# A transformer block on one core: PV in either lane beside the last out projection, first MLP weights in four transfers, second ones later, and another planned order

## The chip, the cores and the metric

The kernel runs on one core of one Trainium2 chip. The metric is device time in microseconds (us) of one execution. The core's engines are named as in the profile: PE (TensorE, matmuls), PEld (its weight loads), ACT (ScalarE), DVE (VectorE), POOL (GpSimd) and SP (SyncE, which mostly issues DMA transfers). Each engine runs its own instruction list in order and waits at semaphores.

## The reference

Input x is 2048 x 512 in bf16. With 32 heads of 16 columns, one key and one value head shared by all of them, and a hidden width of 1792 it computes

```python
xn = layernorm(x)
q, k, v = xn @ wq, xn @ wk, xn @ wv           # q: 32 heads of 16; k, v: one head of 16
p = softmax(q @ k.T * 16 ** -0.5)             # 2048 x 2048 per head
s = concat_heads(p @ v) @ wo
g = silu(silu(xn @ w1) @ w2)
out = x + s * g
```

## The kernel before

A planner written in Python (`Planner`) simulates five engines with fixed costs while the kernel is being built, and writes each engine's instruction list in the order that it finds. Whatever the constants of the planner are, the device only sees the resulting order and the semaphore waits. Some constants are random: `SEEDS` has a number for every 6 us of planned time (`STRETCH`), and each draws other values of the priorities (`Mix`), so another list gives another order of the same kinds of work.

**Work.** The 2048 rows are 16 tiles of 128, or four chunks of 512 queries. The queries of eight heads in a chunk are one block of 128 rows (`qt_sb`, 16 blocks `oi`); a group `g` (32 of them) is four heads of a block, in two pairs `i`. A group has 64 score units, each 64 keys by 512 queries for the two heads of a pair. A unit is a PE step of four matmuls 64x32 (`score`, recorded at L1033 and L1039) into one of the eight PSUM banks. Its exponential is taken either by ACT (L1829, into `pa_sb`, one or two units at once) or by DVE, which writes bf16 bits of an approximation (L1124, into `db_sb`); for the latter three shifted copies are made (POOL at L1311 or DVE at L1307, into `ds_sb`), and their four weighted products with V are added. So an ACT unit needs one PV entry, a DVE unit four. PV (`do_pv`, L1393) collects the group's output and the softmax's sum in one PSUM bank; then DVE transposes, divides and transposes back (`make_norm`, L1414 to L1435) into `on_sb`.

**Lanes.** The 64x32 matmuls of a step take the array's rows in halves of 64; two steps with swapped halves run side by side. The planner calls these lane 0 and lane 1 (`tensor`, mode "U"). A score unit run in one lane has its PV entry fixed to the other lane (`u.lane`, `bt.lanes`), and `pv_half` takes only entries of the lane that asks (L1338).

**MLP.** For each chunk 14 jobs "h" (`mk_h`, products with `w1_sb`, ACT tanh and a DVE product into `u_sb`) and then four jobs "z" (`mk_z`, products of `u_sb` with `w2_sb`). A job's products run in both lanes between scores and PV. Jobs "w" are the out projection of finished chunks; for the last chunk there is a separate end.

**The end.** When all scores are assigned and no job is left, `make_tail` lists for each of four row tiles the first three eight-head blocks of the out projection, once per lane (`tail["half"]`, 12 steps of four matmuls in each lane, L1625). Lane 1 opens the accumulation of a row tile, and lane 0 may only follow when lane 1 has done its three steps for that tile (L1611). The fourth block (L634, full 128 rows) needs the last group's `on_sb` and starts only when lane 0's list is empty (L1635). Then come the products with g (L854 to L859), the sum with x and the stores.

**Transfers.** SP issues nearly all loads in one in-order queue: x tiles, wk, wv, wq, the rest of x, then `w1_sb` in one transfer of 1792 KB once the normalised tile 5 is placed (`W1_AT`, L499), `w2_sb` in 14 transfers of 128 KB, of which number k follows hidden block max(0, k - 3) of chunk 0 (L501), and wo. Between them it copies q (`add_q1`, L771) and V (`mk_V`, L737) to other partitions. The planner takes 250 bytes per ns for transfers (`place`, L182 to L185).

The lines that set which PV entry a lane may run, and when the last block starts:

```python
for ent in pvq[g][i]:
    if ent.lane != lane:
        continue
...
if l == 0 and any(q == r for q, _ in tail["half"][1]):
    return INF
...
if tail["half"][0]:
    return None
```

Of the kernel before, what the change touches and what calls it, by code (L numbers as in the profile page):

```python
# [22 lines left out]
SEEDS, STRETCH = [0, 621430, 964855, 634377, 64350, 0, 694092, 944034, 510981, 983451, 126593, 580856, 234150, 0, 405364, 0, 0, 639952, 236919, 380010, 794098, 385191, 672036, 0, 789095, 553358, 196796, 902258, 0, 0, 0, 514317, 0, 331162, 593301, 0, 0, 437315, 0, 0, 917832, 457243, 378342, 445316, 218187, 875070, 402692, 608418, 665513, 0, 0, 713570, 834070, 919202, 142859, 159991, 0, 53048, 725479, 111780, 0, 961704, 55976, 234814, 688798, 646486, 6388, 105124, 192922, 681295, 882883, 467008, 979031, 477536, 901050, 975096, 0, 0, 980853, 663567, 0, 620538, 913744, 251242, 618568, 299334, 120371, 0, 397467, 0, 362185, 47491, 718084, 0, 0, 0, 0, 0, 635882, 0, 0, 0, 0, 0, 0, 0, 0, 0, 0], 6000.0  # L23
STG = {2: 3, 3: 11}
# [84 lines left out]
class Planner:  # L109
# [47 lines left out]
    def place(self, eng, dur, emit, reads, writes, dma=0, t0=None, ports=1, after=None):  # L157
# [217 lines left out]
def bass_recurrent_scan__grouped_kv_mqa__dense_activation_silu__prompt_kernel(  # L375
# [29 lines left out]
    with ExitStack() as es:  # L405
# [71 lines left out]
        def xkey(t):  # L477
            return ("Ds", XB + t // BS, t % BS)
# [4 lines left out]
        for t in range(4):  # L483
            dma((SP, AC)[t % 2], "x", x_tile(t), xv[:, t, :], 128, [xkey(t)], prio=-2)
        dma(SP, "wk", wkv_sb[:, :, 0:DH], A_wk.rearrange("(dc p) e -> p dc e", p=P), 16, ["wk"], prio=0)
        dma(SP, "wv", wkv_sb[:, :, DH:2 * DH], A_wv.rearrange("(dc p) e -> p dc e", p=P), 16, ["wv"], prio=0)
        dma(SP, "wq", wq_sb[:], A_wq.rearrange("(dc p) n -> p dc n", p=P), 512, ["wq"], prio=0)
        for j in range(1, 4):
            dma(SP, "x", ds_sb[:, XB + 4 * j // BS, 4 * j % BS * NQ:(4 * j % BS + 4) * NQ].bitcast(BF16).rearrange("p (t d) -> p t d", d=D),
                xv[:, 4 * j:4 * j + 4, :], 512, [xkey(4 * j + h) for h in range(4)], prio=1)  # L490
# [80 lines left out]
        for j in range(4):  # L571
            for t in range(4 * j, 4 * j + 4):
                if t == 1:
                    continue
                ts_ = pl.add(Task(DV, 593.0, lambda v, t=t: v.bn_stats(stats_sb[:, t, :], x_tile(t)),  # L575
                                  [xkey(t)], [("st", t)], 1 + j,
                                  gate=(lambda j=j: xn_task[STG[j]].op is not None) if j > 1 else
                                  (lambda: ("xnT", 3) in pl.lastw) if j > 0 else None))
                pl.add(Task(DV, 66.0, lambda v, t=t: v.bn_aggr(mv_sb[:, t, :], stats_sb[:, t, :]),  # L579
                            [("st", t)], [("mv", t)], 1 + j, [ts_]))  # L580
# [242 lines left out]
        def mk_h(c, ft, pace):  # L823
            def consume(jb, op):
# [62 lines left out]
        def add_xr(tt):  # L887
            if tt < NT - 4:
# [4 lines left out]
            xr_task[tt] = pl.add(Task(SP, T_SP, lambda e: e.dma_start(xr_sb[:, tt % 4, :], xv[:, tt, :]),  # L893
                                      (), [("xr", tt % 4), "w1"], 2, [fin_task[tt - 4]], dma=128 * 1024))
            later(xr_task[tt], hidden(NC - 1, NFT - 1))
# [427 lines left out]
        def pv_half(t, lane):  # L1323
# [254 lines left out]

        tail = dict(made=False, items=[], sums=[], half=([], []), prev={})

        def make_tail():
            tail["made"] = True
            c = NC - 1
            for r in range(4):
                tt = 4 * c + r
                for o in range(NOC):
# [16 lines left out]

        def tail_half(l, t):
            if not tail["half"][l]:
# [9 lines left out]
            rr = pl.ready(PE, tail_reads(r, o), [("ps", tb[r])] if o == 0 and l == 1 else ())  # L1615
            if l == 0 and o == 0:
                rr = max(rr, pl.vis(tail["prev"][r], PE))
            if rr > t + 20:
                return rr
            tail["half"][l].pop(0)  # L1620

            def emit(pe):
                for j in range(4):
                    r0 = 64 * (j // 2 ^ l)
                    h = pe.matmul(bank(tb[r])[32 * j:32 * (j + 1), :],  # L1625
                                  lhsT=on_cols(oi % NON, slice(r0, r0 + 64), r * P + 32 * j, 32),
                                  rhs=wo_sb[r0:r0 + 64, o, :], start=o == 0 and l == 1, stop=False,
                                  tile_position=(r0, 32 * j), skip_group_check=True)
                return h
            tail["prev"][r] = pl.tensor("U", l, MM, emit, tail_reads(r, o), [("ps", tb[r])], t,  # L1630
                                        after=tail["prev"].get(r) if l == 0 and o == 0 else None)
# [329 lines left out]
```

## Time and profile before

| | before |
|---|---|
| median of 3 runs | 655.04 us (654.72 to 655.38) |
| the profiled execution's own time | 655.33 us |
| its span | 653.5 us |
| PE, DVE, ACT, POOL busy | 644.5, 632.8, 640.9, 578.6 us |
| first score matmul | 10.34 us |
| last exponential ends | 644.43 us |
| last block of the out projection starts | 647.40 us |
| granted TensorE clock | 1.0 |

The span runs from the first to the last instruction; the execution's time has 1.8 us more around it. A "group" is all instructions of one line, engine and shape. In a row of the timeline the first two numbers are start and length, and the bracket says how long the engine was idle before it and who ended that. "issue" is idle time with no releaser that the profile shows.

### The profile page before, as it was taken

The page shows a single profiled execution, that of the slowest core. Times are in us where ns is not written, and L with a number is a line of the kernel's source. Part 1 is how long each engine was busy: PE and PEld are TensorE (multiplying, and loading weights), DVE is VectorE, ACT ScalarE, POOL GpSimd, SP SyncE. Part 2 cuts the span into 40 slices and gives each one's busy share as a digit, 9 for nine tenths or more (in the row PEclk, how much of TensorE's full clock was granted, in tenths as well). Part 3 has the DMA queues.
Part 4 walks back from the last instruction along what each step waited for, and adds up shares of the span by engine and source line. Part 5 has one row for each costly group of instructions (what it writes and reads, how often), then busy time and mean ns, then how long its engine had stood idle before and what let it go on. Part 6 is the DMA issues. An engine that isn't in the chain of part 4 may idle for free.

```text
span 653.5 us, 44343 instructions
## 1 busy us (share of the span) xinstructions
PE 644.5 (99%) x22007; PEld 347.8 (53%) x19480; DVE 632.8 (97%) x1136; ACT 640.9 (98%) x1132; POOL 578.6 (89%) x331
## 2 busy tenths in 40 slices
PE   7999999999999999999999999999999999999997
PEld 3455656555555554554465555545555555475543
DVE  8999999999999999999999999999999999997995
ACT  7999999999999999999999999999999999999996
POOL 3068899999999999999989999999998999997961
PEclk9999999999999999999999999999999999999999
DMA  6521110000011210000000001000000001200001
GB/s 179 157 66 34 38 42 21 11 5 10 13 35 36 37 34 14 10 5 4 11 5 10 13 13 27 4 5 10 6 10 5 10 14 21 51 4 6 4 3 36
DMA packets 12920, 16.57 MB, mean 25 GB/s; under 512 B 2432, under 2 KB 11904, under 8 KB 12544
## 3 DMA queue, kind: packets, MB, share of 16 engines
q1 hardware_dynamic: 10384, 11.31, 5.9%
q0 software_dynamic: 1920, 2.03, 2.3%
q8 instruction: 162, 2.65, 1.7%
q10 hardware_dynamic: 432, 0.39, 0.2%
q14 instruction: 22, 0.18, 0.1%
HBM read 8.95 MB, written 3.67 MB: 19 GB/s over the span
## 4 chain that ended last, share of the span: by engine, by line
PE 96%; DVE 2%; DMA 1%; SPq 0%; issue 0%
PE ps L1393 33%; PE ps L1039 29%; PE ps L761 20%; PE ps L1033 13%; DMA ds_sb<-in_A_x_dram 1%; DVE stats_sb L575 1%; PE ps L650 1%; PE ps L1625 0%; PE ps L685 0%; SPq L474 0%; PE ps L723 0%; DVE w_sb L856 0%; DVE xn_sb L611 0%; DVE mv_sb L579 0%; DVE w_sb L859 0%
## 5 line engine op out<-in xcount | busy, mean ns | idle before, releaser
L1829 ACT ACTIVATE pa_sb<-ps 128x512 bf16<-128x512 f32 (+1 forms) x1039 | 608.6, 771 | 2.7 <-PE ps L1039 1.9
L1311 POOL INT64_ADD ds_sb<-db_sb x299 | 563.7, 1958 | 33.4 <-PE ps L1393 12.4
L1124 DVE TENSOR_SCALAR db_sb<-ps 128x512 uint16<-128x512 f32 x794 | 494.8, 682 | 6.3 <-PE ps L1039 3.7
L1039 PE MATMUL ps<-qt_sb,kt_sb 64*32 64x512 bf16 x5664 | 481.4, 378 | 1.0 <-ACT pa_sb L1829 0.6
L1393 PE MATMUL ps<-ds_sb,v_sb 64*32 64x512 bf16 x4872 | 359.4, 376 | 0.0
L1393 PE MATMUL ps<-pa_sb,v_sb 64*32 64x512 bf16 x2472 | 258.0, 377 | 0.0
L1033 PE MATMUL ps<-qt_sb,kt_sb 64*32 64x512 bf16 x2528 | 244.2, 375 | 0.8 <-DMA qt_sb<-qt_sb 0.5
L1039 PEld LDWEIGHTS ps<-qt_sb,kt_sb 64*32 64x32 bf16 x5664 | 136.3, 89 | 150.0 <-ACT pa_sb L1829 65.4
L1393 PE MATMUL ps<-db_sb,v_sb 64*32 64x512 bf16 x1624 | 189.5, 376 | 0.0
L1393 PEld LDWEIGHTS ps<-ds_sb,v_sb 64*32 64x32 bf16 x4872 | 140.6, 91 | 41.8 <-issue 12.1
L761 PE MATMUL ps<-xnT_sb,w_sb 64*32 64x512 bf16 x1792 | 133.7, 377 | 0.4 <-issue 0.4
L761 PE MATMUL ps<-w_sb,u_sb 64*32 64x512 bf16 x1792 | 132.7, 377 | 0.0
L1393 PEld LDWEIGHTS ps<-pa_sb,v_sb 64*32 64x32 bf16 x2472 | 87.9, 91 | 28.2 <-issue 10.2
L1393 PEld LDWEIGHTS ps<-db_sb,v_sb 64*32 64x32 bf16 x1624 | 62.1, 91 | 13.0 <-issue 3.4
L761 PEld LDWEIGHTS ps<-xnT_sb,w_sb 64*32 64x32 bf16 x1792 | 44.2, 91 | 24.4 <-issue 6.0
L761 PEld LDWEIGHTS ps<-w_sb,u_sb 64*32 64x32 bf16 x1792 | 44.5, 91 | 17.3 <-issue 4.0
L817 ACT ACTIVATE t_sb<-ps 128x512 bf16<-128x512 f32 x72 | 48.8, 677 | 0.6 <-PE ps L761 0.5
L818 DVE SCALAR_TENSOR_TENSOR u_sb<-t_sb,ps 128x512 bf16<-128x512 bf16 x56 | 38.0, 679 | 0.6 <-ACT t_sb L817 0.2
L761 PE MATMUL ps<-xnT_sb,wq_sb 64*32 64x512 bf16 x480 | 36.1, 377 | 0.0
L761 PE MATMUL ps<-wo_sb,on_sb 64*32 64x512 bf16 x384 | 29.4, 377 | 0.0
L1414 DVE STREAM_TRANSPOSE ps<-ps 128x512 f32<-128x512 f32 (+1 forms) x33 | 23.2, 707 | 4.3 <-PE ps L1393 2.7
L1450 POOL DMA_DIRECT2D kt_sb<-kt_sb x4 | 2.3, 584 | 21.3 <-DVE kt_sb L703 16.0
(79 smaller groups left out, 197.0 us busy)
## 6 DMA issues: line engine op xcount, KB each, us to landing
w_sb<-in_B_w_dram SPq DMA_DIRECT2D x1, 1792.0 KB, 8.9
w_sb<-in_B_w_dram SPq DMA_DIRECT2D x14, 128.0 KB, 2.5
ds_sb<-in_A_x_dram SPq DMA_DIRECT2D x3, 512.0 KB, 6.5
qt_sb<-qt_sb SPq DMA_DIRECT2D x16, 96.0 KB, 2.1
out_dram<-in_A_x_dram SPq DMA_DIRECT2D x12, 128.0 KB, 2.5
out_dram<-ob_sb POOLq DMA_DIRECT2D x12, 128.0 KB, 3.1
v_sb<-v_sb SPq DMA_DIRECT2D x8, 80.0 KB, 2.2
wq_sb<-in_A_wq_dram SPq DMA_DIRECT2D x1, 512.0 KB, 4.6
```

Of the source, the lines that this page charges most:

```text
L575: ts_ = pl.add(Task(DV, 593.0, lambda v, t=t: v.bn_stats(stats_sb[:, t, :], x_tile(t)), [xkey(t)], [("st", t)], 1 + j, gate=(lambda j=j: x ...
L650: h = pe.transpose(dst[:, k, dc * P:(dc + 1) * P], xn_sb[:, t % 4, dc * P:(dc + 1) * P], ident[:, :])
L761: h = pe.matmul(bank(b)[32 * j:32 * (j + 1), :], lhsT=lhs(k, rows, 32 * j, 32), rhs=rhs(k, rows), start=first, stop=last, tile_position=(r ...
L817: t1 = Task(AC, T_AF + 0.8333 * NQ, lambda a: a.activation(t_sb[:, k, :], bank(b), ACT.Tanh, scale=scale), [("ps", b)], [("t", k)], 0)
L818: t2 = Task(DV, T_P, lambda v: v.scalar_tensor_tensor(out=dst, in0=t_sb[:, k, :], scalar=1.0, in1=bank(b), op0=ALU.add, op1=ALU.mult), [(" ...
L1033: h = pe.add_instruction(mybir.InstMatmult(name=pe.bass.get_next_instruction_name(), engine=mybir.EngineType.PE, ins=[pe.lower_ap(q), pe.l ...
L1039: h = pe.matmul(to, lhsT=keys, rhs=q, start=True, stop=True, tile_position=(r0, 32 * j), skip_group_check=True)
L1124: bt.P[k] = pl.add(Task(DV, T_P, lambda v: v.tensor_scalar(db_sb[:, bt.b, k * NQ:(k + 1) * NQ], bank(b), 128.0 * LOG2E, 128.0 * (SHIFT_BET ...
L1311: whole["po"].append(pl.add(Task(PO, 100.0 + (T_P64 - 100.0) * bt.n / BS, lambda g: g.int64_add(ds_sb[:, s, 0:n].bitcast(U64), db_sb[:, bt ...
L1393: h = pe.matmul(bank(OB)[q:q + 32, :], lhsT=lhs(rows), rhs=rhs[rows], start=s0, stop=s1, tile_position=(64 * l, q), skip_group_check=True)
L1414: t1 = pl.add(Task(DV, (T_TR - 60.0) / parts + 60.0, lambda v, cols=cols: v.transpose(bank(OB)[:, cols], bank(OB)[:, cols]), [("ps", OB)], ...
L1829: op = pl.place(AC, 0.8333 * NQ * n + T_AF, lambda a: a.activation(pa3[:, k0:k1 + 1:max(1, k1 - k0), :], ps3[:, b0:b1 + 1:step, :], ACT.Ex ...
```

## The change

1. In the end (`FLEX`), a PV entry may run in either lane once the tail is made. Lane 1 runs out projection steps while they are ready and lane 0 runs PV (`tail["at"]`); when lane 1's remaining steps and the remaining PV are no more than lane 0's steps, the roles are swapped once. Three of the row tiles (`HEADS`) are opened by lane 1 and the fourth by lane 0. The last block waits for both lists.
2. `w1_sb` comes in four transfers of 448 KB, one per block of 128 input columns. They follow normalised tiles 5, 8 and 10 and the K eviction of tile 7. A product round waits only for its own quarter.
3. Transfer k of `w2_sb` follows hidden block 4 + k // 2 of chunk 0.
4. The planner's transfer costs are other ones (360 bytes per ns, other sizes for small loads and V), and wq has another priority behind wk and wv, with the same place in the queue. `SEEDS` is another list of the same length (109), so the whole order is planned anew.

```diff
-W1_AT, SKIP = 5, 1877.999
+W1_AT, SKIP = (5, 8, 10, -7), 1877.999
...
-T_MS, V_AT = 500.0, 9
+T_MS, V_AT, W2_AT, FLEX, HEADS, SW_AT = 500.0, 9, 4, True, 3, 0
...
-T_V, T_VE, V_KB = 220.0, 410.0, 150
+T_V, T_VE, V_KB = 220.0, 410.0, 200
...
-T_SP, T_ST = 600.0, 480.0
+T_SP, T_ST, DMA_RATE, W_KB, WQ_AT, EARLY_ST = 600.0, 480.0, 360.0, 140, 1, 0
+X_KB = 128
...
-                self.dma_t = start + dma / 250.0
-            op.vis = start + dma / 250.0 + 600.0
+                self.dma_t = start + dma / DMA_RATE
+            op.vis = start + dma / DMA_RATE + 600.0
...
-        later(dma(SP, "w1", w1_sb[:], w1v, 1792, ["w1"], prio=2), lambda: xn_task.get(W1_AT))
+        for k in range(NDC):
+            later(dma(SP, "w1", w1_sb[:, k, :], w1v[:, k, :], 448, [("w1", k)], prio=2),
+                  (lambda k=k: xn_task.get(W1_AT[k])) if W1_AT[k] >= 0 else (lambda k=k: evac_kt.get(-W1_AT[k])))
         for k in range(NFT):
-            later(dma(SP, "w2", w2_sb[:, k, :], w2v[:, k, :], 128, [("w2", k)], prio=3), hidden(0, max(0, k - 3)))
+            later(dma(SP, "w2", w2_sb[:, k, :], w2v[:, k, :], 128, [("w2", k)], prio=3), hidden(0, W2_AT + k // 2))
...
-                    lambda k, rows: xnT_sb[rows, k, c * NQ:(c + 1) * NQ], lambda k: ["w1"] + xnT_keys(c))
+                    lambda k, rows: xnT_sb[rows, k, c * NQ:(c + 1) * NQ], lambda k: [("w1", k)] + xnT_keys(c))
...
+            if FLEX and tail["made"]:
+                if lane != tail["at"] and tail_half(lane, t, False) is True:
+                    return t + MM, None
+                rest = sum(max(tot[n, i] - done[n, i] for i in range(2)) for n in range(g, NG))
+                if lane == tail["at"] == 0 and len(tail["half"][1]) + rest <= len(tail["half"][0]) + SW_AT and tail_half(0, t, False) is True:
+                    tail["at"] = 1
+                    return t + MM, None
             for i in range(2):
                 for ent in pvq[g][i]:
-                    if ent.lane != lane:
+                    if ent.lane != lane and not (FLEX and tail["made"]):
                         continue
...
+            if FLEX:
+                tail["half"][0].sort(key=lambda x: (x[0] < HEADS, x[0], x[1]))
...
-            if l == 0 and any(q == r for q, _ in tail["half"][1]):
+            head = int(not FLEX or r < HEADS)
+            if l != head and any(q == r for q, _ in tail["half"][head]):
                 return INF
...
         def tail_round(t):
-            if tail["half"][0]:
+            if any(tail["half"]):
                 return None
```

More of the change, by code (lines that the diff above doesn't have):

```diff
@@ L577, in bass_recurrent_scan__grouped_kv_mqa__dense_activation_silu__prompt_kernel @@
                                   gate=(lambda j=j: xn_task[STG[j]].op is not None) if j > 1 else
-                                  (lambda: ("xnT", 3) in pl.lastw) if j > 0 else None))
+                                  (lambda t=t: ("xnT", 3) in pl.lastw or t < EARLY_ST and xn_task[3].op is not None) if j > 0 else None))
                 pl.add(Task(DV, 66.0, lambda v, t=t: v.bn_aggr(mv_sb[:, t, :], stats_sb[:, t, :]),
@@ L893, in add_xr @@
             xr_task[tt] = pl.add(Task(SP, T_SP, lambda e: e.dma_start(xr_sb[:, tt % 4, :], xv[:, tt, :]),
-                                      (), [("xr", tt % 4), "w1"], 2, [fin_task[tt - 4]], dma=128 * 1024))
+                                      (), [("xr", tt % 4)] + [("w1", k) for k in range(NDC)], 2, [fin_task[tt - 4]], dma=128 * 1024))
             later(xr_task[tt], hidden(NC - 1, NFT - 1))
@@ L1577, in tbk @@
             return tb[r]
-        tail = dict(made=False, items=[], sums=[], half=([], []), prev={})
+        tail = dict(made=False, items=[], sums=[], half=([], []), prev={}, at=0)
         def make_tail():
@@ L1602, in sum_key, with tail_half @@
             return ("fx", r) if r in EVR else ("fin", r % 2)
-        def tail_half(l, t):
+        def tail_half(l, t, go=True):
             if not tail["half"][l]:
@@ L1614, in tail_half @@
                 return INF
-            rr = pl.ready(PE, tail_reads(r, o), [("ps", tb[r])] if o == 0 and l == 1 else ())
-            if l == 0 and o == 0:
+            rr = pl.ready(PE, tail_reads(r, o), [("ps", tb[r])] if o == 0 and l == head else ())
+            if l != head and o == 0:
                 rr = max(rr, pl.vis(tail["prev"][r], PE))
@@ L1619, in tail_half @@
                 return rr
+            if not go:
+                return True
             tail["half"][l].pop(0)
@@ L1626, in emit @@
                                   lhsT=on_cols(oi % NON, slice(r0, r0 + 64), r * P + 32 * j, 32),
-                                  rhs=wo_sb[r0:r0 + 64, o, :], start=o == 0 and l == 1, stop=False,
+                                  rhs=wo_sb[r0:r0 + 64, o, :], start=o == 0 and l == head, stop=False,
                                   tile_position=(r0, 32 * j), skip_group_check=True)
@@ L1630, in tail_half @@
             tail["prev"][r] = pl.tensor("U", l, MM, emit, tail_reads(r, o), [("ps", tb[r])], t,
-                                        after=tail["prev"].get(r) if l == 0 and o == 0 else None)
+                                        after=tail["prev"].get(r) if l != head and o == 0 else None)
             return True
         def tail_round(t):
-            if tail["half"][0]:
+            if any(tail["half"]):
                 return None
```

11 lines of the change are left out of this document (6 added, 5 removed).

## The prediction

> **What bounds the kernel now.** I read the page's busy times and its chain of waits first, then the groups by form, then the windows of 16 us, and last the timeline of both ends.
>
> ```profile
> span 653.5 us, 44343 instructions
> PE 644.5 (99%) x22007; PEld 347.8 (53%) x19480; DVE 632.8 (97%) x1136; ACT 640.9 (98%) x1132; POOL 578.6 (89%) x331
> PE 96%; DVE 2%; DMA 1%; SPq 0%; issue 0%
> L1829 ACT ACTIVATE pa_sb<-ps 128x512 bf16<-128x512 f32 (+1 forms) x1039 | 608.6, 771 | 2.7 <-PE ps L1039 1.9
> L1039 PEld LDWEIGHTS ps<-qt_sb,kt_sb 64*32 64x32 bf16 x5664 | 136.3, 89 | 150.0 <-ACT pa_sb L1829 65.4
> ```
>
> The chain lies 96% on PE, but ScalarE (ACT) is 98% and VectorE (DVE) 97% busy, and the score weights wait longest for exponentials to free a PSUM bank. So three engines bound it together, and a gain must take work or idle time from all of them, or from the ends where only one works.
>
> ```profile
> L1829 ACT ACTIVATE pa_sb<-ps 128x512 bf16<-128x512 f32 x842 | 447.8, 693 | 2.4 <-PE ps L1039 1.9 <-PE ps L1033 0.5
> L1829 ACT ACTIVATE pa_sb<-ps 128x1024 bf16<-128x1024 f32 x197 | 207.2, 1104 | 0.3
> L1124 DVE TENSOR_SCALAR db_sb<-ps 128x512 uint16<-128x512 f32 x794 | 494.8, 682 | 6.3 <-PE ps L1039 3.7 <-PE ps L1033 0.5
> ```
>
> 842 + 2 x 197 = 1236 score units go through ACT, at 608.6 / 1236 = 0.49 us of ACT time each; a unit on DVE costs 494.8 / 794 = 0.62 us. An ACT unit is one PV entry of two matmuls; a DVE unit is four (one plus three shifted copies), so moving a unit to DVE costs PE six matmuls more.
>
> ```profile
> 32.00:48.00 16.00, 15.99 (x480) 7.92 (x428) 15.42 (x28) 14.83 (x27) 10.27 (x7) 1.00 0.22 61
> 240.00:256.00 16.00, 16.00 (x580) 7.68 (x504) 16.00 (x29) 16.00 (x33) 15.77 (x10) 1.00 0.12 21
> 592.00:608.00 16.00, 16.00 (x560) 8.17 (x488) 12.50 (x22) 16.00 (x28) 11.69 (x8) 1.00 0.02 5
> 608.00:624.00 16.00, 16.00 (x572) 9.21 (x495) 14.24 (x26) 16.00 (x30) 14.81 (x8) 1.00 0.02 5
> 624.00:640.00 16.00, 16.00 (x496) 7.04 (x396) 14.42 (x22) 16.00 (x23) 8.28 (x6) 1.00 0.01 3
> ```
>
> After the window come PE, weight loads, DVE, ACT and POOL. The middle is full: 580 matmuls per 16 us (36 per us) with no idle on DVE or ACT. Busy time hides a thin stretch on PE, since two half-arrays run side by side; the counts show it. The weak places are the start (480 matmuls, ACT idle 1.2 us) and the last three windows: DVE is idle 3.5 + 1.8 + 1.6 = 6.8 us, and (580 - 560) + (580 - 572) + (580 - 496) = 112 matmuls are missing, 112 / 36 = 3.1 us of PE. The clock is 1.00 throughout, so no clock effect enters.
>
> **Part 1, PV in either lane beside the out projection.** The end before:
>
> ```profile
> 640.82 3.61 ACT L1829 ACTIVATE pa_sb<-ps 128x1024 bf16<-128x1024 f32 x4
> 642.16 0.40 PE L1625 MATMUL ps<-wo_sb,on_sb 64*32 64x512 bf16 x4
> 644.48 0.10 PEld L1393 LDWEIGHTS ps<-pa_sb,v_sb 64*32 64x32 bf16 x4 [0.26 <-ACT pa_sb L1829]
> 644.55 2.93 PE L1625 MATMUL ps<-wo_sb,on_sb 64*32 64x512 bf16 x52
> 644.94 0.80 DVE L1414 STREAM_TRANSPOSE ps<-ps 128x256 f32<-128x256 f32 x2 [1.59 <-PE ps L1625]
> 646.25 0.49 DVE L1435 STREAM_TRANSPOSE on_sb<-otr_sb 128x128 f32<-128x128 f32 x2
> 647.40 0.56 PEld L634 LDWEIGHTS ps<-wo_sb,on_sb 128*32 128x32 bf16 x16 [0.42 <-issue]
> ```
>
> From 642.16 the out projection (L1625) has one lane and PV the other. The last PV waits for the last exponential (640.82 + 3.61 = 644.43). Then 52 matmuls, 13 steps of four, run one after another in one lane, (2.93 - 0.38) / 12 = 0.21 us each, with the other lane empty. The last round (L634) follows them at 647.40, although its input from DVE was done at 646.25 + 0.49 = 646.74.
>
> ```profile
> 642.40:644.90 2.50, 2.49 (x48) 0.97 (x40) 1.00 0.00 0
> ```
>
> That row is L1393 alone: 48 matmuls, 12 PV steps. With the new rule 12 PV steps and 24 projection steps fill both lanes: 36 x 0.21 / 2 = 3.8 us, done by about 646.0. Then DVE sets L634: 646.74 plus a hand-over of 0.05 (ACT's end at 644.43 to the load at 644.48), so 646.8 in place of 647.4: **-0.6**. More isn't to be had here as long as the last exponential ends where it does, because PV and the DVE chain follow it. The change of lane makes PE wait once for the running step, 0.4 us by L1625's row, and what is queued behind it is both lanes; it is covered while projection steps are left, and costs 0.4 if they are not. Bounds: -0.6 to +0.4.
>
> **Part 2, first MLP weights in four transfers.**
>
> ```profile
> 8.79 1.29 DVE L575 BATCH_NORM_STATS2 stats_sb<-ds_sb 128x6 f32<-128x512 bf16 x2 [0.47 <-DMA ds_sb<-in_A_x_dram]
> 13.34 0.41 PE L1033 MATMUL ps<-qt_sb,kt_sb 64*32 64x512 bf16 x4 [0.53 <-DMA qt_sb<-qt_sb]
> 17.52 0.37 SPq L474 DMA_DIRECT2D w_sb<-in_B_w_dram  x1
> 21.30 0.74 DVE L703 TENSOR_SCALAR kt_sb<-ps,part_sb 128x512 bf16<-128x512 f32 x1
> 23.12 13.14 SPq L737 DMA_DIRECT2D v_sb<-v_sb  x6
> 26.80 0.10 PEld L761 LDWEIGHTS ps<-xnT_sb,w_sb 64*32 64x32 bf16 x4 [0.42 <-DMA w_sb<-in_B_w_dram]
> 31.67 1.58 ACT L1829 ACTIVATE pa_sb<-ps 128x512 bf16<-128x512 f32 x3 [0.24 <-PE ps L1039]
> 33.70 0.09 PEld L1393 LDWEIGHTS ps<-pa_sb,v_sb 64*32 64x32 bf16 x1 [0.50 <-DMA v_sb<-v_sb]
> 34.19 0.60 ACT L1829 ACTIVATE pa_sb<-ps 128x512 bf16<-128x512 f32 x1 [0.94 <-PE ps L1039]
> 35.02 4.51 ACT L1829 ACTIVATE pa_sb<-ps 128x512 bf16<-128x512 f32 x9 [0.23 <-PE ps L1039]
> w_sb<-in_B_w_dram SPq DMA_DIRECT2D x1, 1792.0 KB, 8.9
> w_sb<-in_B_w_dram SPq DMA_DIRECT2D x14, 128.0 KB, 2.5
> wq_sb<-in_A_wq_dram SPq DMA_DIRECT2D x1, 512.0 KB, 4.6
> ```
>
> One transfer, issued at 17.52, lands after 8.9 us, at 26.4, and the first MLP load at 26.80 waits 0.42 for it. Three more issues on SyncE's queue (SP) cost 3 x 0.37 = 1.1 us there; SP has nothing to send between 17.9 and 23.12, so they hide. The last quarter waits for the second K eviction (21.30 + 0.74 = 22.04) and goes ahead of the V copies queued behind it at 23.12; without the gap those would leave up to 1.1 us later. It lands between 22.04 + 0.4 + 2.5 (the 128 KB row) = 24.9 and 22.04 + 0.4 + 4.6 (the 512 KB row) = 27.0; 448 KB is nearest to the 512 KB row, but by then the other quarters can be used and the fourth product round needs the last. So the wait of 0.42 goes: **-0.4**. ACT's gaps at 31.4 to 35.0 (0.24 + 0.94 + 0.23 = 1.4) are PE's, busy with preparation instead of scores; MLP products done earlier would free PE there. Bounds: -0.4 - 1.4 = -1.8, and 27.0 - 26.4 = +0.6 when the product does wait for the last quarter.
>
> The Trainium skill speaks against the split: "DMA: Bandwidth & Descriptors", under Bandwidth, asks for transfers of 1 MiB and more, since smaller ones lose rate. The rows agree in direction (1792 KB at 201 KB/us, 512 KB at 111), and by that rule part 2 would be its upper bound, +0.6, and the sum 1.0 higher.
>
> **Part 3, second MLP weights later and in pairs.**
>
> ```profile
> 40.81 1.77 SPq L474 DMA_DIRECT2D w_sb<-in_B_w_dram  x4
> 86.16 3.20 SPq L474 DMA_DIRECT2D w_sb<-in_B_w_dram  x2
> 98.38 0.61 PE L761 MATMUL ps<-w_sb,u_sb 64*32 64x512 bf16 x8
> ```
>
> The first four leave at 40.81 and would now follow the fifth hidden block; the last one follows block 10 in both versions (13 - 3 = 4 + 13 // 2). The last issue ends by 89.4, lands 2.5 later, and the first use is at 98.38: **0**, hidden by 6 us of other work. Without that cover it would be one landing, 2.5.
>
> **Part 4, the new order.** No row shows it, so I bound it by idle time. If m units of the last three windows move from ACT to DVE, ACT gets shorter by 0.49 m, and PE's missing 3.1 us shrink by 6 m / 36 = 0.17 m. The two meet at 0.49 m = 3.1 - 0.17 m, m = 4.7, a gain of 2.3 us (DVE has room: 4.7 x 0.62 = 2.9 of 6.8). A different order can as well thin out other windows by that much. Bounds -2.3 to +2.3 here; I take half of the possible gain, **-1.2**, because the order fills PE better only in the thin places and cannot in the full windows.
>
> **Sum.** -0.6 - 0.4 + 0 - 1.2 = -2.2. The profiled execution took 655.33 us, 1.8 more than its span; 655.33 - 2.2 = 653.1. The median of the three runs, 655.04, is 0.3 below the profiled one, so I predict **652.8 us**.
>
> **The rivals.** (a) The order gives nothing: the windows from 592 stay as thin, the end alone is repaired, 655.04 - 0.6 - 0.4 = 654.0, or 654.6 if the transfer is hidden anyway. For it: ACT has no idle there, so PE's thin places may be ACT's doing. Against it: DVE idles beside it. (b) Slower: the plan now counts 360 bytes per ns for a transfer in place of 250, so it thinks 512 KB done 2.10 - 1.46 = 0.64 us sooner and puts their consumers earlier. Engine queues run in order, so a consumer that comes too early holds up all behind it. The start has four such waits now: 0.47 (DVE for x), 0.53 (PE for the q copy), 0.42 and 0.50 (PE for weights and V), 1.9 us together. If each grows by 0.64, that is +2.6, and the time 655.04 + 2.6 - 0.6 = 657.0. It decides from the point where these waits pass 1.9 + 1.6 = 3.5 us, the 1.6 being what parts 1 and 4 take less 0.2. For it: all four exist already. Against it: the old rate put 1792 KB at 7.3 us, the trace has 8.9 with everything around it, and the quarters are asked for early. (c) The first product waits for the last quarter, which lands at 27.0 like the 512 KB row: +0.6 in place of -0.4, so 653.8, the same as before within what can be told. For it: the gate at 22.04 is late. Against it: three product rounds can run ahead. This is what the Trainium skill's rule on transfer size would give. (d) The change does not do what it says: the lane rule only acts after all scores are assigned, about 642; if jobs end later than PV, nothing moves and only the order counts, 652.8 + 0.6 = 653.4.
>
> **How the numbers follow.** Forecast with (d) 0.53, (a) 0.14, (b) 0.27, (c) 0.06. The likeliest's own range is 651.0 to 653.7: 655.04 - 0.6 - 0.4 - 2.3 - 0.7 (half of ACT's 1.4) to (d). For 8 in 10 it must reach to (b): from 655.04 - 0.6 - 1.8 - 2.3 - 0.8 = 649.5, the 0.8 for thin windows elsewhere such as 32 to 48, to 657.0 + 1.0 = 658.0, (b) with the end's loss of 0.4 in place of its gain of 0.6. A difference of 0.2% (1.3 us) is about what can be told here from no change, so faster means below 653.7, slower above 656.4. Faster: the forecast and (d), 0.53, and some of (a), 0.03: 0.56. Slower: (b) less its lighter cases, 0.25. Same: 0.19.
>
> **What would show it.** Part 1: L634 starts right behind DVE's last transpose, with PV (L1393) rows in both lanes' places among L1625. Part 2: four w_sb issues between 17 and 23 us, no wait of L761 for w_sb, ACT idle in 31 to 35 below 1.4. Part 3: L761 on u_sb never waits for w_sb. Part 4: more than 1628 matmuls (560 + 572 + 496) in the windows from 592 to 640, and DVE idle below 6.8 there. Wrong if the waits for DMA in the first 40 us pass 3.5 us, if L634 starts as late after the last exponential as now (3.0 us), or if windows in the middle fall below 580.

## The result: slower by 0.46%

| | before | after |
|---|---|---|
| median, same chip | 655.32 us (654.72 to 655.48, 5 runs) | 658.33 us (657.66 to 659.02, 5 runs) |
| ratio | | 1.0046 (95%: 1.0035 to 1.0057) |
| the profiled execution | 655.33 us, span 653.5 | 657.66 us, span 655.8 |
| first product of the first hidden block | 26.80 us | 21.75 us |
| last exponential ends | 644.43 us | 647.36 us |
| last block of the out projection starts | 647.40 us | 649.77 us |

The profile after, first from its page: span, busy times, the chain's shares, and two groups.

```profile
span 655.8 us, 44325 instructions
PE 644.0 (98%) x22006; PEld 340.3 (52%) x19447; DVE 632.1 (96%) x1137; ACT 641.8 (98%) x1139; POOL 580.1 (88%) x332
...
PE 95%; DVE 2%; DMA 2%; SPq 0%; issue 0%
...
L1845 ACT ACTIVATE pa_sb<-ps 128x512 bf16<-128x512 f32 (+1 forms) x1046 | 611.1, 770 | 4.9 <-PE ps L1043 3.5
...
L765 PE MATMUL ps<-xnT_sb,w_sb 64*32 64x512 bf16 x1792 | 136.9, 377 | 2.1 <-DMA w_sb<-in_B_w_dram 2.1
...
w_sb<-in_B_w_dram SPq DMA_DIRECT2D x4, 448.0 KB, 4.3
```

The page looks like the one before: the shares differ by a point. What is new is one releaser, the w1 load, with 2.1 us of PE's idle time behind it, and ACT's idle time ahead of exponentials, 4.9 us for 2.7. So I kept accounts for ACT, which is busy from end to end: its busy time plus its idle time is the span. The windows of before, in five stretches (columns after the window: PE, PEld, DVE, ACT and POOL busy, each with its count, then clock and DMA):

```profile
0.00:16.00 16.00, 12.37 (x204) 5.59 (x200) 13.75 (x62) 12.63 (x25) 6.25 (x17) 1.00 0.61 181
16.00:40.00 24.00, 23.43 (x520) 10.49 (x456) 22.90 (x56) 22.53 (x40) 3.75 (x5) 1.00 0.40 121
40.00:560.00 520.00, 519.62 (x18352) 283.41 (x16257) 516.36 (x882) 519.20 (x929) 502.03 (x274) 1.00 0.08 18
560.00:640.00 80.00, 79.73 (x2734) 44.15 (x2364) 72.24 (x120) 79.53 (x135) 65.28 (x36) 1.00 0.06 12
640.00:662.00 22.00, 9.39 (x237) 4.13 (x212) 7.54 (x19) 6.99 (x11) 1.27 (x1) 0.95 0.08 26
```

The same windows of after:

```profile
0.00:16.00 16.00, 11.76 (x199) 5.24 (x195) 13.50 (x59) 12.12 (x24) 6.24 (x17) 1.00 0.59 180
16.00:40.00 24.00, 20.98 (x452) 8.98 (x380) 20.50 (x54) 20.23 (x34) 1.60 (x3) 1.00 0.42 121
40.00:560.00 520.00, 519.85 (x18304) 277.03 (x16144) 517.04 (x887) 519.64 (x940) 502.10 (x275) 1.00 0.08 17
560.00:640.00 80.00, 80.00 (x2777) 43.71 (x2458) 71.73 (x119) 79.91 (x134) 67.54 (x37) 1.00 0.06 14
640.00:662.00 22.00, 11.38 (x311) 5.34 (x276) 9.37 (x21) 9.92 (x14) 2.58 (x2) 0.96 0.08 27
```

| ACT, us | before | after | difference |
|---|---|---|---|
| idle 0 to 16 (16 less busy) | 3.37 | 3.88 | +0.51 |
| idle 16 to 40 | 1.47 | 3.77 | **+2.30** |
| idle 40 to 560 | 0.80 | 0.36 | -0.44 |
| idle 560 to 640 | 0.47 | 0.09 | -0.38 |
| idle 640 to the end of the span | 6.51 | 5.88 | -0.63 |
| busy in all | 640.88 | 641.82 | +0.94 |
| span | 653.5 | 655.8 | +2.3 |

The loss sits in 24 us, 16 to 40. The first row of the table is no part of the change: x lands later or earlier there from run to run, PE's and ACT's orders are the same in both kernels up to 17 us, and the 3.37 of before is the lowest of five profiles in its order (up to 3.90). The timeline of after shows what happens in the second row: first SP's queue, then the weight loads and matmuls that wait.

```profile
18.13 4.87 SPq L475 DMA_DIRECT2D w_sb<-in_B_w_dram  x4
23.73 14.58 SPq L741 DMA_DIRECT2D v_sb<-v_sb  x6
...
21.75 0.10 PEld L765 LDWEIGHTS ps<-xnT_sb,w_sb 64*32 64x32 bf16 x4 [0.42 <-DMA w_sb<-in_B_w_dram]
24.05 0.40 PE L765 MATMUL ps<-xnT_sb,w_sb 64*32 64x512 bf16 x4 [1.06 <-DMA w_sb<-in_B_w_dram]
27.87 0.40 PE L765 MATMUL ps<-xnT_sb,w_sb 64*32 64x512 bf16 x4 [1.00 <-DMA w_sb<-in_B_w_dram]
```

In the chain of waits of after, one step between the last two is the last quarter, issued at 22.68:

```profile
22.68 5.15 DMA w_sb<-in_B_w_dram
```

A round of the first hidden block is two half-rounds, one in each lane. The new order puts the first six of the eight at 21.75 to 28.5 us; before, the first came at 26.80, behind the single landing. The plan's own price fits these places: 1.4 us, plus 448 KB at 360 bytes per ns (1.27), plus 0.6, is 3.27 us from issue to landing. No run separates that rate from the new `SEEDS`, so which of them moved the half-rounds forward is not shown. The trace has 3.3 for the quickest and 5.1 for the last quarter, with a median of 4.3. PE's queue is in order, so scores stand behind each waiting half-round, and ACT behind them.

The end, from ACT's, DVE's and the weight loads' rows of after:

```profile
635.27 12.09 ACT L1845 ACTIVATE pa_sb<-ps 128x1024 bf16<-128x1024 f32 x13
648.03 0.80 DVE L1425 STREAM_TRANSPOSE ps<-ps 128x256 f32<-128x256 f32 x2 [2.17 <-PE ps L1404]
649.35 0.49 DVE L1446 STREAM_TRANSPOSE on_sb<-otr_sb 128x128 f32<-128x128 f32 x2
649.77 0.55 PEld L638 LDWEIGHTS ps<-wo_sb,on_sb 128*32 128x32 bf16 x16 [0.42 <-DVE on_sb L1446]
```

The last block (now L638) is released by DVE and starts 649.77 - 647.36 = 2.41 us behind the last exponential, where it was 647.40 - 644.43 = 2.97. The thin stretch ahead of it:

```profile
592.00:608.00 16.00, 16.00 (x580) 8.56 (x506) 13.74 (x24) 16.00 (x29) 14.85 (x9) 1.00 0.02 5
608.00:624.00 16.00, 16.00 (x592) 7.41 (x533) 15.76 (x28) 16.00 (x29) 16.00 (x9) 1.00 0.02 5
624.00:640.00 16.00, 16.00 (x501) 7.58 (x408) 13.12 (x20) 16.00 (x21) 10.75 (x7) 1.00 0.01 3
```

1673 matmuls for 1628, and DVE idle for 2.26 + 0.24 + 2.88 = 5.4 us for 6.8: the order fills this stretch a little better.

### The profile page after: what moved, and what is told of

Read it like the earlier page. It is cut to its first block, busy times and chain, and to the rows that moved or that the text cites. A ratio compares the mean times of both kernels' runs of the same rounds, so it can differ in the third digit from the quotient of the medians.

```text
span 655.8 us, 44325 instructions
## 1 busy us (share of the span) xinstructions
PE 644.0 (98%) x22006; PEld 340.3 (52%) x19447; DVE 632.1 (96%) x1137; ACT 641.8 (98%) x1139; POOL 580.1 (88%) x332
## 4 chain that ended last, share of the span: by engine, by line
PE 95%; DVE 2%; DMA 2%; SPq 0%; issue 0%
PE ps L1404 31%; PE ps L1043 29%; PE ps L765 20%; PE ps L1037 13%; DMA ds_sb<-in_A_x_dram 1%; DVE stats_sb L579 1%; DMA w_sb<-in_B_w_dram 1%; PE ps L1641 0%; SPq L475 0%; PE ps L689 0%; DVE xn_sb L615 0%; PE ps L654 0%; DVE xnT_sb L665 0%; DVE kt_sb L707 0%; DVE w_sb L860 0%
## 5 line engine op out<-in xcount | busy, mean ns | idle before, releaser
L1315 POOL INT64_ADD ds_sb<-db_sb x300 | 565.9, 1949 | 32.1 <-DVE db_sb L1128 16.2
L1404 PE MATMUL ps<-pa_sb,v_sb 64*32 64x512 bf16 x2472 | 261.8, 377 | 0.0
L1404 PE MATMUL ps<-db_sb,v_sb 64*32 64x512 bf16 x1624 | 192.2, 377 | 0.0
L1404 PEld LDWEIGHTS ps<-ds_sb,v_sb 64*32 64x32 bf16 x4872 | 138.3, 91 | 42.9 <-issue 14.7
L765 PE MATMUL ps<-xnT_sb,w_sb 64*32 64x512 bf16 x1792 | 136.9, 377 | 2.1 <-DMA w_sb<-in_B_w_dram 2.1
L1404 PEld LDWEIGHTS ps<-pa_sb,v_sb 64*32 64x32 bf16 x2472 | 90.0, 91 | 21.5 <-issue 6.3
L765 PE MATMUL ps<-xnT_sb,wq_sb 64*32 64x512 bf16 x480 | 37.9, 377 | 0.0
```

Of the source, the lines that this page charges most:

```text
L765: h = pe.matmul(bank(b)[32 * j:32 * (j + 1), :], lhsT=lhs(k, rows, 32 * j, 32), rhs=rhs(k, rows), start=first, stop=last, tile_position=(r ...
L1315: whole["po"].append(pl.add(Task(PO, 100.0 + (T_P64 - 100.0) * bt.n / BS, lambda g: g.int64_add(ds_sb[:, s, 0:n].bitcast(U64), db_sb[:, bt ...
L1404: h = pe.matmul(bank(OB)[q:q + 32, :], lhsT=lhs(rows), rhs=rhs[rows], start=s0, stop=s1, tile_position=(64 * l, q), skip_group_check=True)
```

## The experiments

The theory from the trace: half-rounds of the first block stand ahead of their quarters' landings, and that is the loss. Rivals: the split itself, the lane rule, or the rest of the new order. In every run the planned order of all engines was kept as it was, apart from what the edit names. Every ratio is against the kernel before on the same chip; the last column is ACT's idle time from 16 to 40 us in the run's profile, read as above (1.47 before). It comes from one execution, and the ratio from the medians of all. Where an expectation names a run by its short name, the table has it.

| run | ratio, 95% | idle |
|---|---|---|
| the change | 1.0046 (1.0035 to 1.0057) | 3.77 |
| the change again | 1.0046 (1.0034 to 1.0058) | 3.63 |
| quarters behind tile 5 | 1.0023 (1.0010 to 1.0035) | 2.99 |
| quarters ahead of all V copies (q_early) | 1.0047 (1.0030 to 1.0064) | 2.98 |
| one transfer in the new order (q_one) | 1.0106 (1.0086 to 1.0126) | 7.54 |
| the change without the lane rule | 1.0043 (1.0029 to 1.0057) | 5.74 |
| before + lane rule (b_flex) | 0.9992 (0.9983 to 1.0001) | 1.47 |
| before + lane rule, again | 0.9994 (0.9976 to 1.0012) | 1.41 |
| before + four quarters | 1.0015 (1.0004 to 1.0026) | 1.84 |
| before + lane rule, w1 early | 0.9995 (0.9987 to 1.0004) | 1.62 |
| wq for w1 in block 0 | 1.0052 (1.0036 to 1.0067) | 2.91 |
| the same, w1 behind four V copies | 1.0033 (1.0020 to 1.0046) | 3.21 |
| wq in three blocks, w1 behind all V copies | 1.0025 (1.0013 to 1.0036) | 1.88 |
| half-rounds moved | 1.0064 (1.0040 to 1.0087) | 3.78 |
| half-rounds moved, w1 late | 1.0058 (1.0046 to 1.0071) | 4.61 |
| half-rounds moved, quarters behind tile 5 | 1.0031 (1.0014 to 1.0047) | 2.97 |

**When the quarters leave.** Three runs of the new order differ in SP's queue alone, and in what the products then wait for: all four right behind tile 5 (17.85 to 19.6 us), all four far ahead and ungated (11.04 to 13.8), or one transfer behind tile 5. The comments in these lines say where the other two differ.

```diff
+        w1_ops = [t.op for t in w1_tasks]
+        sp = [o for o in pl.order[SP] if o not in w1_ops]
+        at = pl.order[SP].index(w1_ops[0])      # early: 9
+        pl.order[SP] = sp[:at] + w1_ops + sp[at:]
...
+        for o in w1_ops:
+            o.deps = [xn_task[5].op]            # early: []
+        # one transfer: w1_ops[0] loads w1_sb[:], the other three go
```

> The changed kernel in the same order, all four w1 transfers behind normalised tile 5, one behind the other from about 18.1 us. Theory: the bytes themselves need until about 27.0 (before: 8.9 us for all 1792 KB), so the last quarter gains only 0.8 us on the 27.8 of the changed kernel: 657.5 to 658.0. If the gates alone were the loss (transfer rate no limit), the last would land by 18.1 + 1.6 + 4.3 = 24.0 and the time be about 656. Rival 1: 658.3.

> The changed kernel with every engine's order kept; only the four w1 transfers lose their gates and stand on SP right behind the first q copy (about 11 us), so that all have landed by about 20 us. Theory (late quarters: PE, in order, stood 0.42 + 1.06 + 1.00 us at product rounds whose quarter had not landed): no wait of L765 for w_sb, last exponential about 2.1 to 2.6 us earlier, 655.7 to 656.2 us. Rival 1 (the new order as such is worse, and the start is bound by ACT or DVE anyway): the waits go, the time stays within 0.5 of 658.3. Rival 2 (transfers of 448 KB are too slow as such): no difference to theory here, but q_one must then be faster than the changed kernel.

> The changed kernel in the same order, w1 as one transfer of 1792 KB behind tile 5, as it was before. Theory: it lands 8.9 us after 18.1, at 27.0, and the first product round, planned at 21.75, holds PE's queue until then, 5.2 us in place of 2.5 us in three waits: 660 to 661.5. Rival 2 (the split itself is the loss): 656 or less. Rival 1: 658.3 as before.

Behind tile 5 the loss halves, to 1.0023, as the theory had it or a little better; PE's matmuls wait 0.9 us for w1, for 2.1 in the change. Ungated, nothing waits for w1, but the 1792 KB now travel beside the first K and V copies, which take up to 5.2 and 5.1 us to land (medians 2.1 and 2.7), and the weight loads wait 2.0 us for K and 1.8 for V: a wait was moved, not removed, and the run missed its expectation by 2.6 us; its 658.84 is near what rival 1 gave. One transfer is the dearest, 1.5 us above the range that was expected, so in the new order the split is not the loss: it saves (1.0106 - 1.0046) x 655 = 3.9 us. Its waiting row in the timeline, and then its windows (of PE alone):

```profile
26.22 0.61 PE L767 MATMUL ps<-xnT_sb,w_sb 64*32 64x512 bf16 x4 [4.59 <-DMA w_sb<-in_B_w_dram]
```

```profile
24.00:28.00 4.00, 1.78 (x40) 0.55 0.13 47
28.00:32.00 4.00, 4.00 (x64) 0.59 0.20 45
32.00:36.00 4.00, 4.00 (x100) 1.00 0.01 2
```

One half-round at about 21.6 us waits for a load that lands 8.2 us after its issue, and the whole queue stands for 4.59 us. The granted clock then falls to 0.55, so that the next matmuls take 0.61 us for 0.40; the expectation had no clock in it.

**The lane rule alone, with and without the rest.**

Without it, in the new order:

```diff
-T_MS, V_AT, W2_AT, FLEX, HEADS, SW_AT = 500.0, 9, 4, True, 3, 0
+T_MS, V_AT, W2_AT, FLEX, HEADS, SW_AT = 500.0, 9, 4, False, 3, 0
```

Alone, in the kernel before: the `FLEX` lines of the change in `pv_half`, `make_tail`, `tail_half` and `tail_round`, nothing else. The order up to the end stays as it was.

> The kernel before, in its own order up to the end, with the lane rule of the end alone. Theory: 0.6 us less than before, from the last block of the out projection starting right behind DVE's last transpose. Rival: no difference, as the end follows the last exponential.

> The kernel before with the lane rule alone, once more, for the smaller interval: ratio 0.9985 to 0.9995.

> The changed kernel with the lane rule of the end switched off; the order up to the end is the same. Theory: the last block of the out projection waits for projection steps in one lane again, 0.6 us later: 658.9. Rival (the lane rule gives nothing or costs): 658.3 or less.

Rows of ACT and of the weight loads in the timeline of before with the lane rule, at the end:

```profile
635.52 8.14 ACT L1841 ACTIVATE pa_sb<-ps 128x1024 bf16<-128x1024 f32 x9
646.17 0.55 PEld L634 LDWEIGHTS ps<-wo_sb,on_sb 128*32 128x32 bf16 x16 [0.42 <-DVE on_sb L1442]
```

The last block starts 646.17 - 643.66 = 2.51 us behind the last exponential, 0.46 sooner than before. In the timeline of the new order without the rule the same lag is 652.05 - 649.29 = 2.76, 0.35 more than with it:

```profile
635.28 14.01 ACT L1845 ACTIVATE pa_sb<-ps 128x1024 bf16<-128x1024 f32 x15
652.05 0.55 PEld L638 LDWEIGHTS ps<-wo_sb,on_sb 128*32 128x32 bf16 x16 [0.42 <-DVE on_sb L1446]
```

So the rule is worth 0.35 to 0.46 us by the rows, and the lag repeats from profile to profile: in before's order 2.97 without the rule (two profiles) and 2.52 to 2.53 with it (three), in the new order 2.77 without (one) and 2.41 with it (eleven). Both timed runs of it alone lie under the kernel before (0.65 and 0.85 us of median), but neither interval excludes 1; the time of the run without it in the new order says nothing, its interval covers the change's. That run says something else: up to the end it is the same program as the change, and its profile has 5.74 us of idle from 16 to 40 where two profiles of the change have 3.77 and 3.63. So the idle time of a single profile can be 2 us off.

**The split alone, and an earlier single load.** Before's order with the four quarters at the change's gates, each half-round waiting for its own; and before with the lane rule and its one transfer issued ungated at about 16.2 us.

```diff
+        for k, gate in enumerate((xn_task[5].op, xn_task[8].op, xn_task[10].op, evac_kt[7].op)):
...
+            o.emit = lambda e, k=k: e.dma_start(w1_sb[:, k, :], w1v[:, k, :])
+            o.deps = [gate]
...
+                    o.deps = [d for d in o.deps if d is not whole] + ([parts4[w1_round[id(o)]]] if id(o) in w1_round else parts4)
```

> The kernel before in its own order, with w1 in four transfers at the gates of the changed kernel; each product round waits for its own quarter. Theory: in this order the first product round stands at 26.8 and the later ones behind it, so that quarters landing by 27.4 cost at most 0.5 us: 655.3 to 656.1. Rival 2 (the split as such costs): the loss of the changed kernel appears here as well, 657.5 or more.

> The kernel before with the lane rule, and w1 in one transfer without its gate, right behind the first V copies on SP (about 16.2 us in place of 17.5). Theory: it lands 1.3 us sooner, so the wait of 0.42 goes: 0.3 to 0.5 us less than b_flex, 1.0 less than before. Rival (the bytes slow the copies of K and V, as in q_early): 0 to 1 us more than b_flex.

With the half-rounds at before's places the split makes no wait for w1 at all, and yet it costs 1.0015, about 1.0 us, with an interval above 1. Its slowest V copy takes 5.0 us for 3.8 and ACT idles 0.37 us more; the rest isn't located. Taking away before's wait of 0.42 with an earlier load gained nothing (0.9995 against 0.9992), so at its place that wait seems to have been covered by other work.

**wq in w1's place.** These runs ask what the new order would cost without the loads. The block's wait for w1 goes with the edit; in the third run the first three blocks are so changed (`ft > 2`), and in the second and third the four transfers stand later in SP's queue.

```diff
-            product(jb, lambda k, rows, a, n: w1_sb[rows, k, P * ft + a:P * ft + a + n],
+            product(jb, lambda k, rows, a, n: (w1_sb if c or ft else wq_sb)[rows, k, P * ft + a:P * ft + a + n],
```

> The changed kernel in the same order, its transfers and gates unchanged, but the first hidden block of chunk 0 multiplies with wq, which has long been loaded, in place of its columns of w1 (so that block of the output is of other weights), and so waits for no w1 quarter. Theory (the waits of PE's in-order queue for late quarters are the loss): no wait of L765 for w_sb before 36 us, at least 2.5 us less than the changed kernel, 655.4 to 655.9. Rival 1 (the new order itself is the loss): 657.5 to 658.3. In between, the rest above before with the lane rule is what the order costs.

> The changed kernel with the first hidden block multiplied by wq in place of w1 (its output differs), at the new order's own places, and the four w1 transfers behind the V copies. Theory: the 1.16 us wait for V of the earlier run with wq is gone, ScalarE's idle in the first 40 us is 5.0 to 5.8, time 655.2 to 656.4. Rival: the time stays at 657.3 to 658.5.

> The changed kernel with its first three hidden blocks multiplied by wq in place of w1 (the output differs) and the four w1 transfers behind all eight V copies, so that in the first 36 us no byte of w1 moves and nothing waits for it. Theory (w1's bytes and their waits are the whole loss, the order itself costs nothing): ScalarE idle in the first 40 us of 4.8 to 5.4 us as before the change, no wait of PV for V, time 654.6 to 655.8. Rival (part of the loss is the new order's own placing at the start): V and K copies land in 2.0 to 2.3 us, yet idle stays at 5.8 to 6.6 us and the time at 655.9 to 657.2.

The first of them missed: no wait for w1, yet 1.0052, nearer to rival 1's time than to the theory's. Its trace shows in what the theory was too narrow. The quarters still went ahead of the V copies, one of which took 4.4 us to land for a median of 2.2, and PV waited instead (its row in the timeline):

```profile
28.27 0.40 PE L1406 MATMUL ps<-pa_sb,v_sb 64*32 64x512 bf16 x4 [1.16 <-DMA v_sb<-v_sb]
```

Behind four V copies the ratio fell to 1.0033, with 0.49 us of PE's waiting left at that place and a new wait of 0.91 for the next V copies, which now stood behind w1's bytes. With no byte of w1 moving in the first 36 us the windows of the third run are:

```profile
16.00:40.00 24.00, 22.88 (x512) 10.11 (x444) 22.47 (x57) 22.12 (x38) 2.86 (x4) 1.00 0.28 78
40.00:560.00 520.00, 519.07 (x18258) 278.24 (x16096) 515.89 (x884) 519.19 (x936) 501.68 (x275) 1.00 0.08 19
```

ACT's idle time from 16 to 40 us is 24 - 22.12 = 1.88, for 3.77 with w1 and 1.47 before. So by these single profiles 3.77 - 1.88 = 1.9 of the 2.3 us are w1's, its waits and its bytes together, and 0.4 the new order's placing. By its own numbers the rival came nearer in this run: idle in the first 40 us is 3.97 + 1.88 = 5.85, though 0.6 more than before lies ahead of 16 us, where x lands; the V copy at 23.9 still took 3.5 us and PV waited 0.37; and 657.36 stands against 655.9 for the kernel before on that chip. So w1 is most of the idle time that was added from 16 to 40, but less than half of the lost time: (1.0046 - 1.0025) x 655 = 1.4 of 3.0 us by the medians.

**Half-rounds moved.** A repair with the computation whole: the six early half-rounds go to later places where the other lane stands alone.

```diff
+        early = first_h[:6]
+        spots = [pe[n] for n in (117, 121, 122, 124, 125, 125)]
...
+        for o, s in zip(early, spots):
+            pe.remove(o)
+            pe.insert(pe.index(s), o)
...
```

In the late run the four w1 transfers also go behind the fourth V copy, in another one behind tile 5.

> The six half-rounds moved as in the other run, but the w1 transfers where the change has them, ahead of the V copies. Theory: no wait for w1, but one of 0.8 to 1.4 us for V; 0.7 to 1.3 us above the run with the late transfers: 656.2 to 657.3. Rival (w1's bytes ahead of the V copies cost nothing): equal to the run with the late transfers within 0.4 us.

> The changed kernel with its six early half-rounds of the first hidden block moved behind the second pair of V copies' readers, into places where the other lane stands alone, and the four w1 transfers issued behind those V copies. All other orders stay. Theory (the start of the new order is the loss: half-rounds placed before their quarters land, and w1's bytes ahead of the V copies): no product waits for w1, no PV waits for V, ScalarE's idle time in the first 40 us falls from 7.65 us to 5.0 to 5.8, and the time to 655.0 to 656.2. Rival (a gain at the start is lost again later in this order, as it seemed where wq took w1's place): the idle time falls as much, but the time stays at 657.3 to 658.5.

> The changed kernel with the six half-rounds moved and all four w1 transfers behind tile 5's activation (17.9 to 19.6 us). Theory: the quarters land by 25.2, ahead of the moved half-rounds, and the V copies issued at 23.5 find the queues nearly empty: wait for V at most 0.6 us, idle in the first 40 us 5.4 to 6.3, time 655.3 to 656.6. Rival (moving half-rounds costs as much as their waits did): idle over 6.6, time 657.0 or more.

> The changed kernel as it is, as the control on the same chip: 657.6 to 659.0, waits for w1 of 2.0 to 2.6 us on the matmuls.

All three repairs missed. With the transfers where the change has them, PV waits longer for V, as a row of the timeline shows:

```profile
28.65 0.40 PE L1406 MATMUL ps<-pa_sb,v_sb 64*32 64x512 bf16 x4 [1.63 <-DMA v_sb<-v_sb]
```

With the transfers late, the moved half-rounds wait for w1 again, since four quarters issued from 24.9 us on took 5.9 us (median) to land; the timeline of that run:

```profile
32.69 0.40 PE L767 MATMUL ps<-xnT_sb,w_sb 64*32 64x512 bf16 x4 [0.70 <-DMA w_sb<-in_B_w_dram]
34.47 0.40 PE L767 MATMUL ps<-xnT_sb,w_sb 64*32 64x512 bf16 x4 [1.17 <-DMA w_sb<-in_B_w_dram]
```

Behind tile 5 there is little of either (V 0.61 us, w1 nothing), but ACT loses its time elsewhere, at the half-rounds' new place, in the timeline of that run:

```profile
34.51 0.60 ACT L1851 ACTIVATE pa_sb<-ps 128x512 bf16<-128x512 f32 x1 [1.75 <-PE ps L1045]
```

That gap was 0.86 where the half-rounds had not been moved there. Its idle time in the first 40 us, 6.3, came out about as forecast, and the time did not. The control repeats the change's ratio. Across the runs of the new order, the time roughly follows ACT's idle time from 16 to 40: from wq in three blocks to one transfer it is 7.54 - 1.88 = 5.66 us of idle for (1.0106 - 1.0025) x 655 = 5.3 us of time. The other runs lie within 1.2 us of that line, apart from the run without the lane rule, whose profile is one of its slowest executions (659.97 us for a median of 658.68) and lies 2.4 us off. The upper end of the line is no firmer: the profile with one transfer is of that kernel's fastest execution (660.98 for a median of 662.96).

## Why the prediction was wrong

**The steps that failed: part 2, -0.4, and part 4, -1.2, taken as two terms that don't touch each other.** Part 2 said of the last quarter that "by then the other quarters can be used", and took the products to stay where they were, at 26.80. Both fail together. The new order moved the first half-round 5 us forward, onto the first quarter's landing, and the others onto the next ones. The wait of 0.42 did not go: three waits, 0.42, 1.06 and 1.00, took its place. The bound of +0.6 was one landing against another at a fixed place, and that landing was priced too low as well: the last quarter left at 22.68 in place of 22.04 and landed at 27.83, behind the 27.0 of the bound. That the last quarter's gate and the V copies share one queue was seen; that its bytes slow the V and K copies beside them (4.4 and 5.0 us at the slowest, for 3.8 and 4.3 before) was not priced. Part 4 took half of a gain in the thin windows at the end and put nothing into its term for the start, where its new places decide what part 2 costs.

By medians, the new order with no w1 at the start costs (1.0025 - 0.9993) x 655 = 2.1 us, taking the lane rule at the mean of its two runs, where part 4 had -1.2. The loads of w1 at the start add (1.0046 - 1.0025) x 655 = 1.4, where part 2 had -0.4. By the intervals each of the two is good to about 1 us. So the larger miss is part 4's. The traces locate what is w1's, but of the 2.1 us only 0.4 (0.9 with the estimate for ACT's pairing below); the cause of the rest stays open.

The same loads in the two orders say it most plainly. One transfer: 0.9992 in before's order (with the lane rule), 1.0106 in the new one. Four quarters: 1.0015 (without the rule) and 1.0046. The new order is slower with either, by 7.5 and 2.0 us, and the split costs 1.0 us in before's order and saves 3.9 in the new one.

**Rival (b) named the mechanism**, a consumer planned too early that holds up all behind it, with 657.0 for its time; it came to 658.3. Its threshold is read in the waits for DMA in the first 40 us of after:

```profile
PE ps L765 <- DMA w_sb<-in_B_w_dram: 2.1, 2, 1.1
PE ps L1037 <- DMA qt_sb<-qt_sb: 0.2, 1, 0.2
PEld ps L765 <- DMA w_sb<-in_B_w_dram: 3.1, 3, 1.4
DVE stats_sb L579 <- DMA ds_sb<-in_A_x_dram: 1.0, 2, 0.8
ACT pa_sb L567 <- DMA ds_sb<-in_A_x_dram: 0.6, 1, 0.6
```

7.0 us in all (a half-round can be counted twice, at its loads and its matmuls), so well past 3.5; the same count in before gives 2.5 where the prediction counted 1.9. The price was wrong in kind: not 0.64 on each of four waits that existed, but new waits for one load. V and q did not wait longer. The argument against it, that the quarters are asked for early, missed that their consumers are asked for earlier still. A slip in rival (a) changed nothing: without the transfer's gain its time is 655.04 - 0.6 = 654.4, not 654.6.

**Part 4, -1.2.** Its mechanism is there: idle time on ACT from 40 to 640 fell by 0.44 + 0.38 = 0.8 us, the last three windows have more than 1628 matmuls, and DVE idles less than 6.8 there. Two things were left out. The order's own start costs 0.4 (1.88 against 1.47). And I held ACT's work fixed at 0.49 us a unit, while it depends on the pairing. The groups by form after:

```profile
L1845 ACT ACTIVATE pa_sb<-ps 128x512 bf16<-128x512 f32 x856 | 455.1, 698 | 3.9 <-PE ps L1043 3.5 <-PE ps L1404 0.2
L1845 ACT ACTIVATE pa_sb<-ps 128x1024 bf16<-128x1024 f32 x190 | 199.2, 1093 | 1.0 <-PE ps L1037 1.0
```

There are 190 exponentials of two units for 197 before, for the same 842 + 2 x 197 = 856 + 2 x 190 = 1236 units. An estimate from rows: nine single ones in a row took 4.51 us before (0.50 each) and 13 double ones 12.09 after (0.93 each), so seven pairs less cost 7 x (2 x 0.50 - 0.93) = 0.5 us. ACT's busy time rose by 0.94 in the two profiles. That this rise is the order's is not shown: five profiles in before's order give 640.6 to 642.4 us of busy time, twelve in the new one 641.3 to 642.6. Windows in the middle that fall below 580 were to speak against it. One of them after:

```profile
240.00:256.00 16.00, 16.00 (x555) 7.33 (x464) 16.00 (x29) 15.99 (x29) 15.38 (x10) 1.00 0.12 21
```

It cost ACT nothing. Of the 34 windows of 16 us from 48 to 592, 14 are below 580 after, and 16 were so before (555 is the lowest of both), so the sign was badly chosen: 580 was one window's count, and the mean of these 34 was 577 before.

**Part 1, -0.6**, was right in mechanism: L638 is released by DVE. The term was a little large: 0.35 to 0.46 by the rows of single edits. The whole lag shrank by 0.56 in the change; without the rule the new order has 2.77 for before's 2.97, so 0.2 of it is the order's. **Part 3, 0**, holds: no product ever waits for w2. (Two of the first four transfers follow the sixth hidden block, not the fifth; that changes nothing.)

**The Trainium skill's rule** ("DMA: Bandwidth & Descriptors", section Bandwidth), which asks for 1 MiB and more, hardly shows here: issued together behind tile 5, the quarters took 8.8 us from first issue to last landing, the single load 8.2 in the same order and 8.9 in before's. It did not decide: one transfer was the slowest kernel of all, because what counts here is when the first rows land that somebody waits for.

## What to carry to other kernels

A new order and an edit to a transfer are not two terms of a sum: look first at which consumer the new order puts nearest to the load, and price that distance with landing times from the trace under its real neighbours, not with a rate. Whether a split load helps depends on where its consumers stand: here it saved 3.9 us in one order and cost 1.0 in the other. A consumer ahead of its load stalls an in-order queue for every engine fed by it. When three engines are equally busy, keep accounts of busy and idle time by stretch for the one that never rests; it shows in one table where the difference between two executions lies. How much of it is the change's, only medians of many executions tell.

## What was not expected of the hardware

A pause of PE can cost more than its length. After the 4.59 us wait the clock stood at 0.55 to 0.59 for the next two windows of 4 us and matmuls took 0.61 us. In the profile without the lane rule, two waits of 0.80 and 1.69 us 4.7 us apart had the same effect (0.57 from 28 to 32 us), while 1.06 and 1.00 us in the change left it at 1.00. The Trainium skill ("TensorE: Matmul & The Clock Gate", Part 1) puts the fall to half clock at an idle window of about 3.4 us; the long wait agrees, the two short ones are less than the page asks. Whether such pauses widen the scatter from run to run is not shown: on one chip a kernel in the new order ran from 655.97 to 661.57 us, and before's order with the lane rule from 653.94 to 659.68, 12 runs each.

Small copies from SBUF to SBUF were slowed by a big load beside them: the 112 KB K copies from 18 to 40 us all landed in 2.1 us with no w1 moving, and the slowest took 4.3 us beside the single load of before, 5.0 beside the quarters of the change and 5.5 beside the same quarters in before's order. The slowest 80 KB V copy took 3.5 us with no w1 moving, so w1 is not all that slows it, 4.3 to 5.1 with quarters ahead of it that had not landed, and 3.6 and 3.8 where all four quarters had left by 19.2 us. The quarters slow each other as well: a quarter alone at the head took 3.1 to 3.6 us (six runs), four issued together 5.3 to 6.5 (medians of six runs).
